# Two casting transfers in GpSimd's queue in place of eight weight copies on ScalarE, with a new hand-written order

## The chip, the cores and the metric

The kernel runs on one core of a Trainium2 chip. The metric is the device time of one execution in microseconds (us). Three runs of the kernel before took 107.3, 107.71 and 105.91 us; their median is 107.3 us. The engines are called PE (TensorE), DVE (VectorE), ACT (ScalarE), POOL (GpSimd) and SP (SyncE); PEld is PE's weight load.

## The reference

Linear attention with a polynomial feature map (4 batches, 4 heads, 1088 tokens, head dimension 32, r = 8) feeds a two-layer network with a squared ReLU:

```python
def phi(x):
    a = einsum('rd,bhsd->bhsr', S1, x)
    b = einsum('rd,bhsd->bhsr', S2, x)
    return einsum('bhsi,bhsj->bhsij', a, b).reshape(..., 64)
q_p, k_p = phi(q), phi(k)
kv  = einsum('bhsf,bhsd->bhfd', k_p, v)
z   = sum(k_p, axis=2)
num = einsum('bhsf,bhfd->bhsd', q_p, kv)
den = einsum('bhsf,bhf->bhs', q_p, z)[..., None] + 1e-06
x   = (num / den) with heads side by side: 4352 x 128
h   = x @ w_in                    # 128 x 2048
out = maximum(h, 0)**2 @ w_out    # 2048 x 128
```

All inputs and the output are float32.

## The kernel before, in words

The whole kernel is one program of about 490 named operations. A dictionary `ops` holds a function for each name, and the string `ORDER` at the head of the file lists the names; a loop at the end calls them in that order, and `keep` holds the instructions of each engine in it. So each engine runs its instructions in the order of the names, and waits by semaphore where an operand isn't ready. A second table, `BANKS`, gives the PSUM banks of each result. Both tables are written out by hand or by a planner; nothing is decided at run time.

For each batch b (0 to 3) the loads `ld_k`, `ld_q`, `ld_v` bring 544 KB each (k and q of batch 0 in three parts, v in four pieces of 32 partitions and two small rests). The names of the stages, with the lines of the profile:

- `kT`, `qT` (L338 to L341): 32x32 transposes of k and q on DVE. `kP` (L361): PE applies S1 and S2 to k; `kB` (L376): DVE transposes the result back from PSUM.
- `kp` (L381): the products of the two projections, on POOL (`kpP`) or DVE (`kpD`). `KV` (L392): PE sums k_p times v over the tokens; `KVc`, `KVt`, `KVr` (L445, L454, L460) bring that into the form that is used as a weight.
- `G` (L405), `Gc` (L423), `Wv` (L428), `Wd` (L435, L436): a small Gram matrix of the projections, from which the denominator's vector is made. For batch 0 `Ww0` (L438) and `Wc0` (L439) do it in one matrix.
- `qP` (L561; `qPa0` L540 and `qPw0` L548 for the first half of batch 0), `qB` (L571; `qBa0` L552, `qBw0` L555): the projections of q. `aw`, `dr`, `rc`, `an` (L582, L595, L596, L587): the denominator, its reciprocal and the scaled factor. `qp` (L495) and `qf` (L504): the products and their transposes. `xt` (L605) multiplies by kv and `xc` (L624, L625), or `xm` (L646) for the first half batch, writes x as bfloat16.
- The network runs in nine blocks c of 512 tokens (the last has 256). `m1_c_g` (L673) multiplies two of 16 chunks of w_in into a pair of banks, `rlA`/`rlD` (L680, L682) take the maximum with 0 on ACT or DVE, `sq`/`sqA` (L685, L688) square four chunks on DVE or ACT, `m2_c_s` (L700) multiplies four chunks by w_out. `oe` and `od` copy the block out and store it.
- `fill` (L754) issues matmuls of zeros, 384 columns wide.

The weights are loaded in float32 by SP in eight transfers (`ld_wi0` to `3`, L323; `ld_wo0` to `3`, L326) of 256 KB, and copied to bfloat16 tiles by eight ACT copies (`wiA`, L330; `woA`, L331). Their float32 tiles are not their own: `late[0]` and `late[1]` later hold k and q of the batches 2 and 3, and `w_in_f` and `w_out_f` are views of them:

```python
late = [sb(f"late{i}", [128, 2, NJ, D]) for i in range(2)]
k_in += [late[0][:, i] for i in range(2)]
q_in += [late[1][:, i] for i in range(2)]
w_in_f, w_out_f = (t.rearrange(...)[:, : CT * 128]... for t in late)
```

So `ld_k2` waits for the four `wiA`, and `ld_q2` for the four `woA`. The transfers of SP and ACT also share eight completion semaphores in turn: each waits until the eighth before it has landed.

Of the kernel before, what the change touches and what calls it, by code (L numbers as in the profile page):

```python
# [11 lines left out]
ALU = mybir.AluOpType  # L12
# [16 lines left out]
kP2 ld_v3h3 rc2 rlA_1_3 ld_v3r0 sq_0_2 m1_1_4 ld_v3r1 m2_0_1 sqA_1_0 anP2 kB2 ld_q3 m1_1_5 qpP202 qT2 m1_1_6
m2_0_2 rlA_1_4 qpP224 rlD_1_6 KV102 sqA_0_3 KV124 kpP28 KV146 qf2 KV169 qpP302 G2 kT3 KVc1 m1_1_7 qpP324 Gc2  # L30
rlA_1_5 Wv2 m2_0_3 kT3r kpP202 WdA2 qf3 rlA_1_7 qP4 KVt1 oeA0 kpP268 qB41 kP3 KVr1 od0 qB40 sqA_1_1 xt2 kB3
awP4 qT0r kpP38 dr4 G3 xcA20 rc4 m2_1_0 xcD21 Gc3 anP4 sqA_1_2 sq_1_3 m1_2_0 m1_2_1 m1_2_2 qT2r qpP502 rlA_2_0
qT1r rlD_2_1 m2_1_1 qpP524 rlA_2_2 m1_2_3 qT3 m1_2_4 kpP224 m1_2_5 rlA_2_4 m2_1_2 rlD_2_3 kpP246 rlA_2_5
m1_2_6 m1_2_7 sq_2_0 rlA_2_6 m2_1_3 rlA_2_7 m1_3_0 qpP424 oeD1 m1_3_1 rlD_3_0 Wv3 od1 m1_3_2 kpP324 rlA_3_1
m2_2_0 qf5 rlA_3_2 qpP402 m1_3_3 m1_3_4 WdA3 rlA_3_3 sq_2_1 m1_3_5 KV202 rlA_3_4 KV224 kpP346 qf4 KV246 KV269
qP6 KVc2 rlA_3_5 KVt2 qB60 m2_2_1 KVr2 qB61 sqA_3_2 xt4 sq_2_2 sq_2_3 m1_3_6 xcA40 m2_2_2 xcA41 awD6 rlA_3_6
sq_3_0 m1_3_7 m1_4_0 rlA_3_7 m1_4_1 dr6 m2_2_3 rc6 sqA_3_1 qT3r rlD_4_1 m1_4_2 m2_3_0 anD6 sq_3_3 rlA_4_0
m1_4_3 m2_3_1 rlA_4_2 qpP724 rlD_4_3 m1_4_4 sqA_4_0 m2_3_2 kpP302 rlD_4_4 m1_4_5 kpP368 m1_4_6 rlD_4_5 m1_4_7
rlA_4_6 m2_3_3 qpP702 oeD2 rlA_4_7 m1_5_0 qpP624 od2 qf7 m1_5_1 rlA_5_0 m1_5_2 KV302 sq_4_1 rlA_5_1 KV324
KV346 KV369 rlA_5_2 oeD3 m1_5_3 qpD602 od3 m1_5_4 rlA_5_3 m1_5_5 sq_4_2 m2_4_0 KVc3 qf6 KVt3 m1_5_6 KVr3  # L40
m2_4_1 rlA_5_5 rlD_5_4 m2_4_2 rlA_5_6 sq_4_3 m1_5_7 sqA_5_2 xt6 sq_5_0 m2_4_3 xcA61 xcD60 rlA_5_7 sq_5_1
m1_6_0 m1_6_1 oeA4 m1_6_2 rlA_6_0 rlD_6_1 od4 m2_5_0 rlA_6_2 m1_6_3 sq_5_3 m1_6_4 rlA_6_3 m1_6_5 rlD_6_4
m2_5_1 rlA_6_5 m1_6_6 sq_6_0 m1_6_7 m1_7_0 rlA_6_7 rlD_6_6 m2_5_2 m1_7_1 sq_6_1 rlA_7_0 m2_5_3 rlA_7_1 sq_6_3
# [747 lines left out]
```

## Time and profile before

| | |
|---|---|
| median of three runs | 107.3 us |
| profiled execution, its own time | 107.26 us |
| its span (first to last recorded instruction) | 104.9 us |
| busy: PE, DVE, ACT, POOL | 96.0, 90.4, 83.6, 40.1 us |
| read from HBM, written | 8.79 MB, 2.23 MB |
| granted PE clock | 1.00 |

The span is 2.4 us shorter than the execution's time; what lies around it is not in the trace. "Busy" of PE is modelled from pipelined matmuls, so a busy PE need not be PE at its peak. In rows of the timeline stand the start (us), the duration (us), the engine, the line, the operation, the result and operands with their shapes, and in brackets the idle time before and what ended it. "x18" counts instructions; a float32 matmul is recorded as two.

### The profile page before, as it was taken

Reading aid. Unit: us, or ns where it says so; the run is one execution under the profiler, and the core shown is the slowest. Engines: PE = TensorE matmul, PEld = TensorE weight load, DVE = VectorE, ACT = ScalarE, POOL = GpSimd, SP = SyncE. Lnnn points to the kernel's source line nnn. Section 1 sums busy time; section 2 is a strip of 40 time slices with the busy share of each in tenths; the row PEclk is TensorE's granted clock in tenths of the full one; section 3 lists DMA queues with packets and bytes.
Section 4 is the critical chain, followed back from the end, with each engine's and each line's share of the span. In section 5 each row is a group of like instructions: output and inputs, shape, how many; then the busy total and the mean of one; then the engine's idle time right before and its main releaser. Section 6 shows DMA issues by size and latency. Waiting matters only on the chain.

```text
span 104.9 us, 4069 instructions
## 1 busy us (share of the span) xinstructions
PE 96.0 (91%) x1771; PEld 69.7 (66%) x1771; DVE 90.4 (86%) x133; ACT 83.6 (80%) x105; POOL 40.1 (38%) x52
## 2 busy tenths in 40 slices
PE   2999988998889996999999999999999999999960
PEld 1436755555358853778777778877877787889950
DVE  3486598999993999999899999999999999995920
ACT  0720458499999988899999999998999799969920
POOL 4063011597099982899950008940000000210000
PEclk9999999999999999999999999999999999999999
DMA  1998999599999844000130000034102200040423
GB/s 47 284 262 289 261 395 256 104 315 232 214 254 176 198 86 112 9 0 0 31 75 6 0 6 0 0 75 99 32 6 48 52 6 0 0 106 0 103 51 106
DMA packets 9649, 11.28 MB, mean 107 GB/s; under 512 B 2592, under 2 KB 6816, under 8 KB 9632
## 3 DMA queue, kind: packets, MB, share of 16 engines
q1 hardware_dynamic: 8976, 10.59, 40.3%
q10 hardware_dynamic: 656, 0.43, 1.4%
q8 instruction: 14, 0.23, 0.9%
q14 instruction: 3, 0.02, 0.1%
HBM read 8.79 MB, written 2.23 MB: 105 GB/s over the span
## 4 chain that ended last, share of the span: by engine, by line
PE 67%; DMA 12%; DVE 9%; ACT 4%; issue 4%; SPq 0%; DVEq 0%
PE banks L700 26%; PE banks L673 23%; DMA late<-in_q_dram 8%; PE banks L605 6%; DMA k_in<-in_k_dram 3%; DVE qf L504 2%; PE banks L754 2%; PE banks L392 2%; ACT rg L680 2%; PE banks L405 2%; PE banks L361 1%; DVE qp L495 1%; DVE rg L682 1%; DVE kT L340 1%; ACT w_out_sb L331 1%
## 5 line engine op out<-in xcount | busy, mean ns | idle before, releaser
L680 ACT ACTIVATE rg<-banks 128x1024 bf16<-128x1024 f32 x50 | 48.5, 1039 | 3.2 <-PE banks L673 3.1
L673 PE MATMUL banks<-xT,w_in_sb 128*128 128x512 bf16 (+1 forms) x144 | 35.6, 371 | 0.7 <-DVE rg L682 0.4
L700 PEld LDWEIGHTS <-rg 128*128 128x128 bf16 x544 | 32.5, 98 | 5.5 <-issue 1.1
L700 PE MATMUL banks<-w_out_sb,rg 128*128 128x128 bf16 x544 | 35.3, 219 | 0.4 <-ACT rg L680 0.4
L495 POOL TENSOR_TENSOR qp<-an,qab 128x512 f32<-128x512 f32 x14 | 17.4, 1261 | 31.5 <-DVE an L587 31.3
L685 DVE TENSOR_TENSOR rg<-rg 128x2048 bf16<-128x2048 bf16 x21 | 26.0, 1250 | 0.0
L673 PEld LDWEIGHTS <-w_in_sb 128*128 128x128 bf16 x144 | 17.9, 146 | 8.2 <-issue 2.8
L682 DVE TENSOR_SCALAR rg<-banks 128x1024 bf16<-128x1024 f32 x18 | 21.6, 1209 | 1.6 <-PE banks L673 1.3
L688 ACT ACTIVATE rg<-rg 128x2048 bf16<-128x2048 bf16 x11 | 21.2, 1927 | 0.0
L381 POOL TENSOR_TENSOR kp<-kab 128x512 f32<-128x512 f32 (+1 forms) x17 | 16.2, 969 | 4.2 <-DVE kab L376 4.2
L504 DVE STREAM_TRANSPOSE qf<-qp 128x1024 f32<-128x1024 f32 (+1 forms) x9 | 10.5, 1167 | 0.0
L754 PE MATMUL banks<-zfill 128*128 128x384 bf16 x26 | 7.7, 416 | 2.0 <-POOL zfill L207 2.0
L605 PE MATMUL banks<-qf,KVr 32*32 32x256 f32 (+2 forms) x384 | 7.5, 323 | 0.8 <-DVE qab L571 0.8
L605 PEld LDWEIGHTS banks<-qf,KVr 32*32 32x32 f32 x384 | 4.7, 103 | 2.8 <-ACT KVr L460 1.3
L571 DVE STREAM_TRANSPOSE qab<-banks 128x512 f32<-128x512 f32 (+2 forms) x10 | 5.2, 550 | 0.5 <-PE banks L561 0.5
L582 POOL TENSOR_TENSOR aw<-qab 128x256 f32<-128x256 f32 (+1 forms) x3 | 1.9, 637 | 8.3 <-DVE qab L571 8.3
L754 PEld LDWEIGHTS <-zfill 128*128 128x128 bf16 x26 | 2.6, 121 | 3.5 <-POOL zfill L207 2.0
L392 PEld LDWEIGHTS banks<-kp,v_in 128*32 128x32 f32 x256 | 4.2, 116 | 0.9 <-issue 0.4
L330 ACT CAST w_in_sb<-late 128x512 bf16<-128x512 f32 x4 | 2.3, 620 | 3.0 <-DMA late<-in_moe_w_in_dram 3.0
L392 PE MATMUL banks<-kp,v_in 128*32 128x64 f32 x256 | 4.6, 227 | 0.0
L405 PEld LDWEIGHTS banks<-kab 128*64 128x64 f32 x72 | 3.1, 158 | 1.5 <-DVE kab L376 0.6
L340 DVE STREAM_TRANSPOSE qT<-late 128x1024 f32<-128x1024 f32 x2 | 2.5, 1240 | 1.8 <-DMA late<-in_q_dram 1.8
(84 smaller groups left out, 78.1 us busy)
## 6 DMA issues: line engine op xcount, KB each, us to landing
out_dram<-osb SPq DMA_DIRECT2D x32, 64.0 KB, 1.7
v_in<-in_v_dram SPq DMA_DIRECT2D x14, 128.0 KB, 8.0
late<-in_k_dram SPq DMA_DIRECT2D x2, 544.0 KB, 7.8
late<-in_q_dram SPq DMA_DIRECT2D x2, 544.0 KB, 7.8
late<-in_moe_w_in_dram SPq DMA_DIRECT2D x4, 256.0 KB, 4.3
late<-in_moe_w_out_dram SPq DMA_DIRECT2D x4, 256.0 KB, 8.3
k_in<-in_k_dram SPq DMA_DIRECT2D x1, 544.0 KB
q_in<-in_q_dram SPq DMA_DIRECT2D x1, 544.0 KB, 4.0
```

The source lines that it names most:

```text
L381: keep(eng.tensor_tensor(out=kp[i][:, m0:m1].rearrange("p m h i j -> p (m h) i j"), in0=a[:, :, :, None].to_broadcast([128, 4 * n, 8, 8]), ...
L392: keep(pe.matmul(ps[32 * h : 32 * h + 32, 0:64], v_in[b][:, h, m, :] if m < 8 else v_re[b][:, h, :], kp[i][:, m, h].rearrange("p i j -> p ...
L495: keep(eng.tensor_tensor(out=qp[i3][:, k0:k1].rearrange("p m h i j -> p (m h) i j"), in0=a[:, :, :, None].to_broadcast([128, 4 * nn, 8, 8] ...
L504: keep(dve.transpose(dst.rearrange("p g m t -> p m g t"), qp[i3][:, :n].rearrange("p m h i j -> p m (h i j)").rearrange("p m (g d) -> p m ...
L605: keep(pe.matmul(ps[:, 0:N], KVr[b if g < 8 else hi][32 * hi : 32 * hi + 32, e, 32 * h : 32 * h + 32], f[32 * hi : 32 * hi + 32, 2 * h + e ...
L673: keep(pe.matmul(y, w_in_sb.rearrange("p a b -> p (a b)")[:, per * g + z :: CT], xv, start=True, stop=True))
L680: keep(act.activation(o, pair(f"H{c}_{g}"), ACTF.Relu))
L682: keep(eng.tensor_scalar_max(o, pair(f"H{c}_{g}"), 0.0))
L685: keep(dve.tensor_tensor(out=rgs(s), in0=rgs(s), in1=rgs(s), op=ALU.mult))
L688: keep(act.activation(rgs(s), rgs(s), ACTF.Square))
L700: keep(pe.matmul(bank(f"O{c}")[:, 128 * z : 128 * z + 128], gtile(ct)[:, 128 * z : 128 * z + 128], w_out_sb[:, ct, :], start=(ct == 0 and ...
L754: keep(pe.matmul(P8[:, b, 0:384], zfill[:, 0:128], zfill, start=True, stop=True))
```

## The change

The weights are cast on the way in, by one transfer each, issued from POOL's queue straight into the bfloat16 tiles; the eight loads, the eight copies and the two views are gone:

```diff
-    for p in range(4):
-        cs = slice(4 * p, 4 * p + 4)
-        for tag, eng in (("ld", sp), ("ald", act)):
-            ops[f"{tag}_wi{p}"] = lambda cs=cs, eng=eng: keep(eng.dma_start(
-                out=w_in_f[:, cs], in_=moe_w_in.rearrange("d (ct c) -> d ct c", c=128)[:, cs]
-            ))
...
-        ops[f"wiA{p}"] = lambda cs=cs: keep(act.copy(w_in_sb[:, cs], w_in_f[:, cs]))
-        ops[f"woA{p}"] = lambda cs=cs: keep(act.copy(w_out_sb[:, cs], w_out_f[:, cs]))
+    ops["pld_wi"] = lambda: keep(pool_e.dma_start(
+        out=w_in_sb, in_=moe_w_in.rearrange("d (ct c) -> d ct c", c=128)
+    ))
+    ops["pld_wo"] = lambda: keep(pool_e.dma_start(
+        out=w_out_sb, in_=moe_w_out.rearrange("(c ct) d -> c ct d", ct=CT)
+    ))
```

The Gram matrix is made of 18 smaller matmuls for each batch, in four column groups instead of two, and its tile halves:

```diff
             for m in range(9):
-                c = m % 2
-                y = kab[i][:, m].rearrange("p r d -> p (r d)")
-                keep(pe.matmul(
-                    ps[64 * c : 64 * c + 64, 0:32], y, y.rearrange("p (h u i) -> p h u i", u=2, i=r)[:, :, 0],
-                    start=(m < 2), stop=(m >= 7),
-                ))
+                for rr_ in range(2):
+                    c = 2 * (m % 2) + rr_
+                    y = kab[i][:, m, rr_]
+                    keep(pe.matmul(
+                        ps[32 * c : 32 * c + 32, 0:16], y, y.rearrange("p (h u i) -> p h u i", h=2, u=2)[:, :, 0],
+                        start=(m < 2), stop=(m >= 7),
+                    ))
```

`fill` takes a width as well (26 fills of 384 columns become 21 of 128, 256 or 384), a form of the ReLU that no name of the order uses is added (`rlQ`), and `ORDER` and `BANKS` are new throughout. The head of the two orders, up to the first matmul of the network:

```diff
-c_id c_hm ald_S0 ld_k00 ald_S1 ld_k01 c_E c_pk c_z ald_k0r ld_v0h0 c_pW ald_v0h2 fill1b0 fill4b1 ld_v0h1 c_tab
-ald_v0h3 kT00 c_Wp fill1b2 ld_q00 ld_v0r0 c_W kP00 ld_v0r1 kT01 c_W4 ld_wi0 kT0r c_Wq kB00 kP01 ld_wi1 kpP002
-c_S2p fill2b6 kB01 c_S2c ld_wi2 G0 fill2b6 kpD024 c_pv ld_wi3 kpD046 c_eps ld_q01 Gc0 Wv0 Ww0 fill2b6 kpP08
-ld_q0r qT00 ld_k1 kpD068 qPa0 ld_wo0 Wc0 ld_wo1 qPw0 qBa0 ld_wo2 KV002 WdD0 qpD002 KV024 KV046 qpD024 ld_wo3
-wiA2 KV069 fill5b3 wiA1 qBw0 qf0 awP0 KVc0 wiA0 ld_v1h0 KVt0 fill5b3 wiA3 dr0 ld_v1h1 qT01 rc0 ld_v1h2 qP1
-rrbA KVr0 qB10 rr qB11 xt0 fill2b2 ld_v1h3 kT1 awP1 rrc kT1r xm0 ld_v1r0 woA0 kP1 xm1 dr1 m1_0_0 rc1 ld_v1r1
+c_id c_hm ald_S0 ld_k00 ald_S1 ld_k01 c_E c_pk c_z ald_k0r ld_v0h0 ald_v0h2 c_pv fill1b0w128 fill7b1w256
+ld_v0h1 c_tab c_eps ald_v0h3 kT00 c_Wp fill2b2w256 ld_q00 ld_v0r0 c_pW c_W kP00 fill1b4w256 ld_v0r1 kT01 c_W4
+pld_wi kT0r c_Wq kB00 kP01 ld_q01 kpP002 c_S2p fill4b6w256 kB01 c_S2c ld_q0r kpD024 ld_k1 pld_wo KV002 kpD046
+ld_v1h0 G0 kpP08 ld_v1h1 qT00 KV024 ld_v1h2 Gc0 kpD068 Ww0 ld_v1h3 qPa0 Wc0 Wv0 qBa0 qPw0 ld_v1r0 qT01 qpP024
+KV046 KV069 ld_v1r1 WdD0 qBw0 qP1 KVc0 awD0 qpP002 KVt0 fill6b1w384 dr0 qB10 rc0 KVr0 qB11 rrbA qf0 awP1 rr
+fill1b7w384 rrc dr1 xt0 fill3b0w384 rc1 kT1r ld_q1 anP1 kT1 qpP124 xm0 kP1 qpP102 xm1 qT0r m1_0_0 kB1 m1_0_1
```

Behind that, by the counts of the names: ReLUs on ACT 50 and then 51, on DVE 18 and then 17; squares of four chunks on ACT 11 and then 10, on DVE 21 and then 22; products `qp` on DVE for three names (`qpD002`, `qpD024`, `qpD602`) and then one (`qpD802`); `aw` on DVE for the groups 6 and 8 and then for group 0. `Wv` and `Ww0` read the smaller tile of the Gram matrix.

More of the change, by code (lines that the diff above doesn't have):

```diff
@@ L29 @@
[L29 to L33, printed above, removed]
@@ L39 @@
[L39 to L43, printed above, removed]
@@ L126 @@
     q_in += [late[1][:, i] for i in range(2)]
-    w_in_f, w_out_f = (
-        t.rearrange("p b j d -> p (b j d)")[:, : CT * 128].rearrange("p (ct c) -> p ct c", c=128) for t in late
-    )
     v_in = [sb(f"v_in{b}", [128, H, 8, D]) for b in range(4)]
@@ L136 @@
     KVs = [sb(f"KVs{i}", [128, 2, 4, 32]) for i in range(2)]
-    Gs = [sb(f"Gs{i}", [128, 32]) for i in range(2)]
+    Gs = [sb(f"Gs{i}", [128, 16]) for i in range(2)]
     KVr = [sb(f"KVr{b}", [128, 2, 128]) for b in range(4)]
@@ L437, in mk_k @@
         if b == 0:
-            ops["Ww0"] = lambda: keep(pe.matmul(bank("GW0")[:, 96:128], S2blk, Gs[i], start=True, stop=True))
+            ops["Ww0"] = lambda: keep(pe.matmul(bank("GW0")[:, 96:128], S2blk, Gs[i][:, None, :].to_broadcast([128, 2, 16]), start=True, stop=True))
             ops["Wc0"] = lambda: keep(dve.tensor_tensor(
@@ L682, in rl, with rl2 @@
                 keep(eng.tensor_scalar_max(o, pair(f"H{c}_{g}"), 0.0))
+        def rl2(g):
+            a, bb = BANKS[f"H{c}_{g}"]
+            o = rgt(g)
+            o = o if a < bb else o[:, ::-1]
+            keep(dve.tensor_scalar(o, pair(f"H{c}_{g}"), 0.0, 2.0, ALU.max, ALU.pow))
         def sq(s):
@@ L749, with fill @@
         mk_f(c)
-    def fill(n, b):
+    def fill(n, b, w):
         for _ in range(n):
-            keep(pe.matmul(P8[:, b, 0:384], zfill[:, 0:128], zfill, start=True, stop=True))
+            keep(pe.matmul(P8[:, b, 0:w], zfill[:, 0:128], zfill[:, 0:w], start=True, stop=True))
     for name in ORDER:
         if name.startswith("fill"):
-            fill(*[int(x) for x in name[4:].split("b")])
+            fill(*[int(x) for x in name[4:].replace("b", "w").split("w")])
         else:
```

60 lines of the change are left out of this document (34 added, 26 removed).

## The prediction

> **What bounds the kernel now.** I read the page first, for the shares and the slices.
>
> ```profile
> span 104.9 us, 4069 instructions
> ...
> PE 96.0 (91%) x1771; PEld 69.7 (66%) x1771; DVE 90.4 (86%) x133; ACT 83.6 (80%) x105; POOL 40.1 (38%) x52
> ...
> DVE  3486598999993999999899999999999999995920
> ACT  0720458499999988899999999998999799969920
> ...
> DMA  1998999599999844000130000034102200040423
> ```
>
> Each slice is 2.6 us. The DMA engines are full from the second slice to about 36 us; VectorE (DVE) and ScalarE (ACT) are full from about 20 us to 95 us. So there is a front part ruled by arrival and a short dependent chain, and a long part in which TensorE (PE), DVE and ACT are all full. Which of the three rules is told by the chain of work that ended last, in order of time.
>
> ```profile
> 25.20 8.87 DMA late<-in_q_dram
> ...
> 40.82 1.49 PE banks L605 x60
> 42.30 0.70 PE banks L405 x18
> 43.00 1.00 PE banks L700 x16
> ...
> 97.67 3.59 PE banks L700 x64
> 101.28 0.37 ACT osb L744
> ```
>
> From 40.82 to 101.28 us every piece of the chain is PE: 60.5 us without a hole. The last row gives 3.59 us for 64 matmuls, 56 ns for 128 columns, the same rate as everywhere else in it (16 in 0.9 to 1.0 us). This stretch gets shorter only if PE has less to do in it. Anything else must come from before 40.8 us, and there PE is not the limit:
>
> ```profile
> 0.00:5.00 5.00, 2.94 (x16) 1.33 (x24) 1.99 (x14) 1.72 (x4) 1.28 (x8) 1.00 0.59 157
> 5.00:10.00 5.00, 4.83 (x65) 2.49 (x61) 4.08 (x8) 1.07 (x7) 2.58 (x8) 1.00 1.03 283
> 10.00:15.00 5.00, 5.00 (x112) 3.29 (x111) 3.55 (x9) 2.55 (x5) 0.46 (x1) 1.00 0.94 312
> ...
> 20.00:25.00 5.00, 4.83 (x82) 3.04 (x85) 4.89 (x7) 4.79 (x7) 5.00 (x6) 1.00 0.82 261
> 25.00:30.00 5.00, 3.79 (x94) 2.31 (x84) 5.00 (x8) 5.00 (x7) 1.83 (x3) 1.00 1.10 201
> 30.00:35.00 5.00, 5.00 (x99) 3.53 (x100) 3.15 (x5) 5.00 (x6) 4.83 (x6) 1.00 0.95 200
> ```
>
> The columns are PE, PEld, DVE, ACT, POOL busy, then the granted clock, the DMA share and GB/s. From 20 to 35 us ACT is busy 14.8 of 15 us and DVE 13.0, nearly all of DVE's gap lying in one window. The waits name that gap, and what SyncE's queue waits for:
>
> ```profile
> DVE qT L340 <- DMA late<-in_q_dram: 1.8, 1, 1.8
> ```
>
> ```profile
> SPq L293 <- DMA late<-in_k_dram: 1.9, 1, 1.9
> ...
> SPq L293 <- ACT w_out_sb L331: 1.4, 1, 1.4
> ```
>
> **The change, term by term.** *The start.* The first MoE matmul (L673) starts at 19.09 us. The timeline on the way to it:
>
> ```profile
> 7.46 1.28 PE L405 MATMUL banks<-kab 128*64 128x32 f32 x18
> ...
> 9.65 0.64 PE L438 MATMUL banks<-Gs,S2blk 128*128 128x32 f32 x2
> ...
> 10.10 0.83 PE L754 MATMUL banks<-zfill 128*128 128x384 bf16 x2
> ...
> 10.86 0.68 PE L540 MATMUL banks<-qT,W 64*32 64x128 f32 x16
> ...
> 12.13 1.29 DVE L495 TENSOR_TENSOR qp<-qab 128x512 f32<-128x512 f32 x2
> ...
> 13.34 0.31 DVE L555 STREAM_TRANSPOSE qw<-banks 128x128 f32<-128x128 f32 x1
> ...
> 13.73 0.46 POOL L582 TENSOR_TENSOR aw<-qab,qw 128x128 f32<-128x128 f32 x1 [4.86 <-DVE qw L555]
> ...
> 14.70 0.26 DVE L595 TENSOR_REDUCE den<-aw 128x16 f32<-128x144 f32 x1
> 14.88 0.70 DVE L339 STREAM_TRANSPOSE qT<-q_in 128x512 f32<-128x512 f32 x1
> 15.50 0.21 DVE L596 RECIPROCAL rec<-den 128x16 f32<-128x16 f32 x1
> ...
> 16.89 1.20 DVE L340 STREAM_TRANSPOSE kT<-k_in 128x1024 f32<-128x1024 f32 x1
> ...
> 18.15 0.72 DVE L646 TENSOR_TENSOR xT<-banks,recr 128x256 bf16<-128x256 f32 x2
> ...
> 19.09 1.08 PE L673 MATMUL banks<-xT,w_in_sb 128*128 128x512 bf16 x4
> ```
>
> In the new order Wv0 and the fills no longer stand ahead of Ww0 and qPa0 (L540), while KV002 now stands ahead of G0; together I take qPa0 at 9.8 instead of 10.86. The two qp products (1.29 us) leave DVE for POOL, where they delay only qf0, and qT01 (0.70) moves into their place: qBw0 (L555) goes from 13.34 to about 11.8. aw moves from POOL to DVE and qf0 no longer stands between aw and dr0: dr0 from 14.70 to 12.4. Then qB10 takes the place of qT01, and rc0 falls from 15.50 to about 13.1: 2.4 us earlier. qf0, xt0 and kT1 follow on DVE and PE as before (kT1, 1.20 us, stands ahead of xm0 in both kernels), and since DVE now has qB11, qf0 (about 1.2), dr1, rc1, kT1r and kT1 in a row from 13.3, xm0 comes at 16.6 and L673 at 17.6. That is 1.5 us earlier, if k of batch 1 has landed by about 15.2, when DVE reaches kT1r. An earlier start does not need w_in sooner than 17.6, 14 us after its transfer is issued.
>
> Here the transfers decide. By the three windows, 157, 283 and 312 GB/s over 5 us each, 3.76 MB have come by 15 us. Up to and with k1 the queue of before holds k, v and q of batch 0, w_in and k1: four times 0.56 MB and 1.05 MB, 3.3 MB, by these rates in by 13.6 us. Afterwards both weights start early (w_in at about 3 us behind POOL's memsets, w_out behind kpP002, about 7.3) and run beside SP's queue. If all 2.1 MB get ahead of k1, it is 4.3 MB before k1: at 250 to 300 GB/s beyond 15 us that is 17 us, kT1r, kT1, xm and the first matmul follow, and L673 starts at 19.4. So the term lies between -1.5 and +0.3; I take the middle, -0.6, since w_out's second half comes late enough to fall behind k1.
>
> The same engines then carry v0 and q00 more slowly between 4 and 10 us; KV002, put ahead of G0 on PE, would hold G0 behind v0. In the worst case (w_in's 1.05 MB at 283 GB/s, 3.7 us, all in front, less what the old order already had there) qPa0 returns to about 11.8 and L673 to the same 19.4, so this is inside the same bounds and is not added.
>
> *POOL.* Each transfer costs POOL its issue. No row shows one; the nearest is SP's:
>
> ```profile
> 5.32 2.45 SPq L323 DMA_DIRECT2D late<-in_moe_w_in_dram  x4
> ```
>
> That is 0.6 us each, so I bound one between 0.3 and 2 us. Behind pld_wi waits kpP002, whose input comes only at 6.1 us: covered. Behind pld_wo waits kpP08, which only KV069 needs, some microseconds later: 0, and up to +0.5 if an issue takes 2 us. SP loses eight issues, and with them eight places among the transfers it may have open.
>
> *The eight ACT copies.*
>
> ```profile
> 17.59 1.14 ACT L331 CAST w_out_sb<-late 128x512 bf16<-128x512 f32 x2
> ...
> 24.04 1.14 ACT L331 CAST w_out_sb<-late 128x512 bf16<-128x512 f32 x2
> ```
>
> Only the pair at 24.04 lies where ACT is full; the other six lie before 20 us beside an idle ACT and are worth 0. So 1.14 us of ACT, out of 8 x 0.6.
>
> *The late loads.* q of batch 2 is issued at 25.20 because SP waits 1.4 us for w_out's last copy; it lands 8.87 us later, and DVE stands 1.8 us. The change removes the 1.4, but 8.87 us is mostly the queue (share 1.10 and 0.95 in the windows), and k3's wait (1.9 us) is for a transfer, not for a copy, so it stays. The landing moves by 0 to 2.5 us; I take 1.4 of DVE's 1.8 as won. Relu and squares can go to either engine and both are full, so PE gets its food earlier by half of the sum: (1.14 + 1.4) / 2 = 1.3. Bounds 0.6 and 1.5.
>
> *Work moved by the new order behind 20 us.*
>
> ```profile
> L680 ACT ACTIVATE rg<-banks 128x1024 bf16<-128x1024 f32 x50 | 48.5, 1039 | 3.2 <-PE banks L673 3.1
> ...
> L685 DVE TENSOR_TENSOR rg<-rg 128x2048 bf16<-128x2048 bf16 x21 | 26.0, 1250 | 0.0
> L682 DVE TENSOR_SCALAR rg<-banks 128x1024 bf16<-128x1024 f32 x18 | 21.6, 1209 | 1.6 <-PE banks L673 1.3
> L688 ACT ACTIVATE rg<-rg 128x2048 bf16<-128x2048 bf16 x11 | 21.2, 1927 | 0.0
> ```
>
> By the order's names ACT gets one relu more and one square fewer (+1.04 - 1.93), DVE one relu fewer and one square more (-1.21 + 1.25), and about 1 us of products (qpD602 at half of the 1.29 above, aw6) goes from DVE to POOL: 1.9 us off the two, 0.95 each. If PE rules throughout it is worth 0, if they rule 0.95. I take half, 0.5.
>
> *PE.* G becomes 18 small matmuls of 16 columns instead of 9 of 32. In the 43-us row above 16 issues of L700 take 1.0, and a G takes 0.70 for 18 issues; 36 issues could cost from 0.6 to 1.1 us. Two lie in the full stretch: -0.2 to +0.8, taken as 0. Fewer fills: taken as 0, with up to +0.6 (L438's 0.64 doubled) if PE ran slower for lack of them.
>
> *The sum.* -0.6 - 1.3 - 0.5 = -2.4 us. The profiled execution took 107.26 us for a span of 104.9, so 2.4 us lie around it; the median of the three runs is 107.3. Forecast: span 102.5, time 104.9 us. With every term at its best end it is -1.5 - 1.5 - 0.95 - 0.2 = -4.1, 103.2; at its worst +0.3 - 0.6 + 0.5 + 0.8 + 0.6 = +1.6, 108.9.
>
> **Rivals.** *A, interleaving eats the start.* Both weights pass ahead of k1. For it: the DMA share is already 1.03 and 0.94 from 5 to 15 us, so 2 MB pushed in there must delay something; against it: w_out is issued only after 7 us. Then +0.3 - 1.3 - 0.5 = -1.5: 105.8 us, no difference. The Trainium skill states this mechanism as a rule (DMA: Bandwidth & Descriptors, "Queues, rings and completion order"): each engine alternates between the queue rows it has work for, a packet at a time, so a second issuing engine adds no bandwidth. No run here shows two filled queues of different packet sizes yet; by that rule, with long weight rows against the 512 B pieces of q00, the sum would be A's 105.8 and not 104.9.
>
> *B, a casting transfer is slow: slower than before.* A transfer that narrows the type might move at half the rate. No row shows one. For 2.1 MB at 150 GB/s on engines that are already full, 7 us more of engine time stand ahead of q1, k2 and v1, some 4 of them ahead of k1. With 4 us of delay on A's 17 us L673 starts at 23.4: +4.3, less 0.8 for the ACT copies and half of the moved work, is +3.5, 110.8 us. It decides (over 2% slower, +2.1) from the point where L673 starts after 22.0, which is k1 landing after 19.6. Against it: w_out is not needed before the first squares, near 27 us.
>
> *C, the order is worth more.* k1 lands early, so that the start takes its best end (0.9 us more than summed), and 1.1 of the 1.4 us that PE's windows from 20 to 35 us leave empty (13.6 busy of 15) are filled: 102.9. For it: DVE and ACT have less to do there; against it: they stay full.
>
> *D, the late loads do not move at all*, since each also waits for a transfer issued before it: then the 1.4 is lost and 105.6 is left. I count it with A.
>
> **How the numbers follow.** Forecast 0.42, with its own range 103.6 to 106.2; A and D 0.20; B 0.20; C 0.18. Two per cent of 107.3 is 105.2 below and 109.4 above, about what a measurement of this kernel can tell from no change. The forecast lies just past that line, so I give it 0.26 faster and 0.16 same; with C that is 0.44 faster, with A and D 0.36 same, and B is 0.20 slower. The range reaches from 102.0 (C and a little) to 109.5 (B's milder part, and past the sum's worst end), leaving out about 0.1 above and 0.08 below.
>
> **What would show it.** Right: L673 first between 17.6 and 19.4 us; no CAST of ACT before it; DVE's wait on late q under 1 us; PE unbroken from about 39 us; G at 0.6 to 0.9 us. Wrong: kT of batch 1 waiting on k_in (A, B), weights landing after 16 us (B), holes in PE's chain after 41 us (then the new order, not PE's work, sets the end), or PE's part after 41 us shorter by more than 1 us.

## The result and the profile after

The changed kernel took 111.28 us (median of four runs, 109.34 to 113.29) beside 107.39 us for the kernel before (four runs). The ratio is 1.029, with a 95% interval of 1.020 to 1.037: slower, where 104.9 us and a gain were forecast. A ratio here compares the runs of each kernel that lie close to its fastest, a median is over all its runs, and a profile is of one run, whose own time stands in the table below: what is read from a profile far above its kernel's fastest run need not hold for the ratio. The profiled run took 110.51 us for a span of 108.7, so 1.8 us lie around the span (2.4 before).

The page of the changed kernel, its span, PE's clock and the DMA share in 40 slices, and the two queues that matter (packets, MB, share of 16 engines):

```profile
span 108.7 us, 4176 instructions
...
PEclk9999555599999999999999999999999999999996
DMA  2999999999960000210030000003400031200341
...
q0 software_dynamic: 288, 1.05, 5.0%
...
q8 instruction: 14, 0.23, 0.8%
```

Before, PEclk was 9 throughout; now it is 5 in four slices, from about 11 to 22 us. The loads are all in after 12 slices, 33 us, where before they lasted to about 41. PE's own timeline says where the 3.8 us of span went:

```profile
9.63 0.43 PE L382 MATMUL banks<-kp,v_in 128*32 128x64 f32 x16 [1.80 <-DMA v_in<-in_v_dram]
...
12.25 0.68 PE L531 MATMUL banks<-qT,W 64*32 64x128 f32 x16 [1.20 <-DVE qT L328]
...
16.51 0.74 PE L552 MATMUL banks<-qT,Wq 32*32 32x128 f32 x32 [1.75 <-DVE Wq L427]
...
17.66 2.13 PE L753 MATMUL banks<-zfill 128*128 128x384 bf16 x6
19.58 1.06 PE L626 MATMUL banks<-ident,rec 128*128 128x128 f32 x4
...
23.33 2.38 PE L664 MATMUL banks<-xT,w_in_sb 128*128 128x512 bf16 x9
...
31.74 0.47 PE L382 MATMUL banks<-kp,v_in 128*32 128x64 f32 x17 [1.57 <-issue]
```

The first matmul of the network (L664, before L673) starts at 23.33 us instead of 19.09: 4.24 us late. From it to the last piece of the chain it is 104.60 - 23.33 = 81.3 us, where before it was 101.28 - 19.09 = 82.2. So in this profile the whole loss lies in the start, and behind it 0.9 us are won; the end from that piece on is 0.5 us longer (4.1 beside 3.6).

```profile
...
5.41 10.26 DMA q_in<-in_q_dram
...
17.87 1.92 PE banks L753 x6
...
53.06 2.86 ACT rg L671 x3
55.92 1.80 ACT rg L686
...
59.95 2.98 ACT rg L671 x3
62.95 1.91 ACT rg L686
...
104.60 0.37 ACT osb L743
```

The longest row of the chain names the start's cause in this run: the second part of q of batch 0 (q01) is issued at 5.41 us and takes 10.26 us to come. DVE stands for both parts, q00 and q01; the first row is the kernel before, where q00 was in time at 8.31 us:

```profile
8.31 0.70 DVE L338 STREAM_TRANSPOSE qT<-q_in 128x512 f32<-128x512 f32 x1
```

```profile
11.48 0.71 DVE L328 STREAM_TRANSPOSE qT<-q_in 128x512 f32<-128x512 f32 x1 [2.47 <-DMA q_in<-in_q_dram]
...
15.69 0.71 DVE L329 STREAM_TRANSPOSE qT<-q_in 128x512 f32<-128x512 f32 x1 [2.20 <-DMA q_in<-in_q_dram]
...
17.74 0.21 DVE L587 RECIPROCAL rec<-den 128x16 f32<-128x16 f32 x1
```

What shared the engines with it is seen in the DMA view from 2 to 18 us, where the two casting transfers (q0) hold a third of the 16 engines, and in POOL's timeline, which shows when they were issued:

```profile
q1 hardware_dynamic: 3768, 2.60, 60.9%
q0 software_dynamic: 288, 1.05, 33.7%
...
w_in_sb<-in_moe_w_in_dram POOLq DMA_DIRECT2D x1, 512.0 KB, 8.0
q_in<-in_q_dram SPq DMA_DIRECT2D x2, 256.0 KB, 8.9
```

```profile
2.83 0.72 POOL L316 DMA_DIRECT2D w_in_sb<-in_moe_w_in_dram  x1
...
7.21 0.59 POOL L319 DMA_DIRECT2D w_out_sb<-in_moe_w_out_dram  x1
```

The parts of q took 8.9 us (middle of the two) from issue to landing; before it was 4.2. In the trace a packet of the casting queue is 4096 bytes and took 299 ns of an engine on average, one of the 512-byte packets of SP's queue 29 ns. With little to do from 8 us on, PE also lost its clock (the columns are those of the prediction's windows: PE, PEld, DVE, ACT, POOL busy, then the granted clock, the DMA share, GB/s):

```profile
10.00:15.00 5.00, 3.52 (x131) 2.52 (x118) 1.84 (x4) 0.35 (x2) 1.43 (x2) 0.61 1.03 259
15.00:20.00 5.00, 3.49 (x42) 2.11 (x43) 4.14 (x13) 1.08 (x3) 1.19 (x3) 0.50 0.97 236
20.00:25.00 5.00, 4.95 (x95) 2.80 (x95) 3.47 (x6) 1.57 (x3) 3.06 (x4) 0.87 1.05 273
...
30.00:35.00 5.00, 3.38 (x104) 2.34 (x94) 4.22 (x6) 3.61 (x6) 0.72 (x2) 1.00 0.38 111
```

At 0.50 the six fills take 2.13 us and `rr` (L626) 1.06; before, `rr` (L635) took 0.66. A last thing is new: at 30.17 us PE stops inside a group of matmuls for 1.57 us, and the trace shows nothing that it waits for ("issue").

### The profile page after: what moved, and what is told of

It reads as the page before. It is cut to its first block, busy times and chain, and to the rows that moved or that the text cites. A ratio compares the mean times of both kernels' runs of the same rounds, so it can differ in the third digit from the quotient of the medians.

```text
span 108.7 us, 4176 instructions
## 1 busy us (share of the span) xinstructions
PE 94.4 (87%) x1827; PEld 69.7 (64%) x1843; DVE 90.6 (83%) x129; ACT 78.7 (72%) x98; POOL 43.8 (40%) x57
## 3 DMA queue, kind: packets, MB, share of 16 engines
q0 software_dynamic: 288, 1.05, 5.0%
## 4 chain that ended last, share of the span: by engine, by line
PE 65%; DMA 12%; ACT 12%; issue 4%; SPq 1%; DVE 1%
PE banks L698 25%; PE banks L664 23%; DMA q_in<-in_q_dram 9%; ACT rg L671 6%; PE banks L596 6%; ACT rg L686 3%; PE banks L753 3%; DMA k_in<-in_k_dram 3%; PE banks L552 2%; PE banks L351 2%; PE banks L382 1%; PE banks L445 1%; PE banks L396 1%; SPq L303 1%; ACT xT L615 1%
## 5 line engine op out<-in xcount | busy, mean ns | idle before, releaser
L664 PE MATMUL banks<-xT,w_in_sb 128*128 128x512 bf16 (+1 forms) x128 | 33.9, 372 | 0.9 <-ACT rg L671 0.3
L683 DVE TENSOR_TENSOR rg<-rg 128x2048 bf16<-128x2048 bf16 x22 | 27.6, 1273 | 0.0
L664 PEld LDWEIGHTS <-w_in_sb 128*128 128x128 bf16 x144 | 17.6, 147 | 7.0 <-issue 2.0
L673 DVE TENSOR_SCALAR rg<-banks 128x1024 bf16<-128x1024 f32 x17 | 20.4, 1209 | 0.6 <-PE banks L596 0.4
L371 POOL TENSOR_TENSOR kp<-kab 128x512 f32<-128x512 f32 (+1 forms) x17 | 17.9, 1079 | 4.8 <-DVE kab L366 4.8
L686 ACT ACTIVATE rg<-rg 128x2048 bf16<-128x2048 bf16 x10 | 19.1, 1940 | 0.1
L486 POOL TENSOR_TENSOR qp<-an,qab 128x512 f32<-128x512 f32 x14 | 15.6, 1140 | 5.8 <-DVE an L578 5.6
L573 POOL TENSOR_TENSOR aw<-qab 128x256 f32<-128x256 f32 (+2 forms) x5 | 3.8, 768 | 32.6 <-DVE qab L562 32.6
L753 PE MATMUL banks<-zfill 128*128 128x256 bf16 (+2 forms) x26 | 7.5, 427 | 2.1 <-POOL zfill L203 2.0
L436 ACT COPY KVs<-banks 128x256 f32<-128x256 f32 x4 | 1.4, 385 | 5.4 <-PE banks L382 5.4
L552 PE MATMUL banks<-qT,Wq 32*32 32x256 f32 (+2 forms) x160 | 3.4, 360 | 1.8 <-DVE Wq L427 1.8
L366 DVE STREAM_TRANSPOSE kab<-banks 128x576 f32<-128x576 f32 (+2 forms) x5 | 3.3, 663 | 1.8 <-PE banks L351 1.8
```

The source lines that it names most:

```text
L371: keep(eng.tensor_tensor(out=kp[i][:, m0:m1].rearrange("p m h i j -> p (m h) i j"), in0=a[:, :, :, None].to_broadcast([128, 4 * n, 8, 8]), ...
L486: keep(eng.tensor_tensor(out=qp[i3][:, k0:k1].rearrange("p m h i j -> p (m h) i j"), in0=a[:, :, :, None].to_broadcast([128, 4 * nn, 8, 8] ...
L664: keep(pe.matmul(y, w_in_sb.rearrange("p a b -> p (a b)")[:, per * g + z :: CT], xv, start=True, stop=True))
L673: keep(eng.tensor_scalar_max(o, pair(f"H{c}_{g}"), 0.0))
L683: keep(dve.tensor_tensor(out=rgs(s), in0=rgs(s), in1=rgs(s), op=ALU.mult))
L686: keep(act.activation(rgs(s), rgs(s), ACTF.Square))
```

## The experiments

Theory 1: the early casting transfers take engine time from q and v of batch 0, whose arrival the new order has on its path. Rivals: the casting itself is slow; the new order is slow by itself; the low clock is the cause and not a consequence. A second theory came from the first runs: PE stops because the next piece of its own program comes late. Each profile gave a start of the network, the stops of PE of 0.5 us or more, and a length from that start to the last piece of the chain, the last copy. The column "profile" has the profiled run's own time and its mean granted clock:

| kernel | median us (runs) | ratio, 95% | profile: us, clock | network starts | PE's stops ("issue") | start to last copy |
|---|---|---|---|---|---|---|
| before | 107.39 (4) | | 107.26, 1.00 | 19.09 | none | 82.2 |
| after | 111.28 (4) | 1.029 [1.020, 1.037] | 110.51, 0.94 | 23.33 | 1.57 | 81.3 |
| e1_late_weights | 107.73 (10) | 1.000 [0.995, 1.005] | 108.67, 0.97 | 19.91 | 1.87, 1.85 | 82.8 |
| e2_before_cast | 108.99 (4) | 1.015 [1.012, 1.019] | 109.08, 1.00 | 21.57 | 0.93 | 81.4 |
| e3_plain_weights | 108.72 (10) | 1.002 [0.996, 1.009] | 110.94, 0.97 | 20.45 | 0.94, 2.00 | 85.1 |
| e4_no_weights | 109.14 (10) | 0.998 [0.991, 1.005] | 109.08, 0.96 | 22.29 | 2.65, 1.27 | 81.0 |
| e5_fills | 109.25 (4) | 1.023 [1.014, 1.033] | 108.49, 1.00 | 21.03 | 0.99, 0.65, 0.92 | 81.6 |
| e6_plain_pool | 109.34 (4) | 1.025 [1.014, 1.036] | 109.21, 0.97 | 22.38 | 0.51 | 81.3 |
| e7_later_wout | 109.34 (4) | 1.015 [1.004, 1.026] | 110.05, 0.97 | 20.83 | 2.69, 1.65 | 83.3 |
| e8_before_late_cast | 107.15 (10) | 1.007 [1.003, 1.010] | 106.28, 1.00 | 19.11 | none | 81.0 |
| e9_old_gram | 108.73 (4) | 1.016 [1.009, 1.023] | 108.25, 0.97 | 17.84 | 1.38 | 84.3 |
| e10_only_win_early | 112.07 (4) | 1.048 [1.042, 1.053] | 111.87, 0.98 | 21.91 | 0.72, 2.35 | 84.1 |
| e11_few_fills | 108.43 (10) | none (see there) | 108.73, 0.97 | 18.64 | 1.47, 2.69 | 84.2 |
| e12_no_late_loads | 106.13 (12) | 0.994 [0.988, 1.000] | 105.94, 1.00 | 19.01 | none | 81.0 |

The kernel before was run again beside each group of kernels, and the ratios are to these runs: its medians were 107.54 us (e1, e2, e3, e5), 106.94 (e4, e6, e7, e8), 106.80 (e9, e10, e11) and 107.62 (e12).

**Late weights.** The two casting transfers only move back in POOL's queue, to about 8.6 and 13 us:

```diff
-pld_wi kT0r c_Wq kB00 ... ld_k1 pld_wo KV002 kpD046
+kT0r c_Wq kB00 ... ld_k1 KV002 kpD046
-kpP08 ld_v1h1 ... qpP002 KVt0
+kpP08 pld_wi ld_v1h1 ... qpP002 pld_wo KVt0
```

> The changed kernel with the two casting transfers later in POOL's order: w_in behind kpP08 (about 8 us) instead of ahead of kpP002 (2.8 us), w_out behind qpP002 instead of ahead of kpP08 (7.2 us). Theory 'starved inputs' (the casting transfers share the DMA engines with v0, q00 and q01, which the start needs first): q00 lands near 8 us and q01 near 10 instead of 11.5 and 15.7, the first matmul of the network (L664) starts between 17.6 and 19.0 instead of 23.3, PE's granted clock stays at 1.0, and the time is 105 to 107. Rival 'order' (the new order is slow by itself: KV002 ahead of G0, qT01 on the way to rc0, fewer fills): L664 still after 21 and the time 109.5 or more.

The time went back to that of the kernel before (1.000), though neither it nor the start reached the ranges expected. q00 and q01 were transposed at 9.01 and 10.70 us without a wait, and `rc0` came at 13.40 where the prediction's chain had 13.1:

```profile
10.70 0.67 DVE L328 STREAM_TRANSPOSE qT<-q_in 128x512 f32<-128x512 f32 x1
...
13.40 0.21 DVE L586 RECIPROCAL rec<-den 128x16 f32<-128x16 f32 x1
```

So the early place of the two transfers was the cause of the loss, and the chain on DVE had been worked out rightly up to `rc0`. Yet the network began at 19.91, not at 17.6. PE's timeline:

```profile
13.84 0.40 PE L551 MATMUL banks<-qT,Wq 32*32 32x128 f32 x3 [1.87 <-issue]
...
14.45 1.89 PE L752 MATMUL banks<-zfill 128*128 128x384 bf16 x6
16.13 1.06 PE L625 MATMUL banks<-ident,rec 128*128 128x128 f32 x4
...
19.91 1.30 PE L663 MATMUL banks<-xT,w_in_sb 128*128 128x512 bf16 x4
```

PE stopped for 1.87 us three matmuls before the end of the projections `qP1`, and then ran six fills in 1.89 us in front of `rr`, at a granted clock of 0.69 from 15 to 20 us. The one packet of the program's queue in the DMA view from 10 to 15 us took 1.8% of 16 x 5 us, 1.4 us; it landed at 12.42 us, and PE went on at 13.84:

```profile
q8 instruction: 1, 0.02, 1.8%
```

**The casting alone, in the old order**, at the same early places of POOL's queue:

```diff
-c_z ald_k0r
+c_z c_pv c_eps pld_wi ald_k0r
-kpP002 c_S2p
+kpP002 pld_wo c_S2p
-(ld_wi0 to 3, ld_wo0 to 3, wiA0 to 3, woA0 to 3)
```

> The kernel before, in its own order, with only the weights changed: the eight loads and eight copies are gone and the two casting transfers stand in POOL's queue where the changed kernel has them (2.8 us, behind the memsets, and behind kpP002). 'Starved inputs': q00 lands near 11.5 instead of 8.1, so qPa0 moves from 10.9 to 12.3; q01 lands at 15.7, when the old order wants it at 14.9; L673 starts at 20.5 to 21.5 instead of 19.1 and the time is 107.5 to 109.5. 'Order': no harm from the transfers, L673 at 19.1 or sooner and 105.5 to 106.5.

It costs 1.5% here, and 108.99 us is in the range expected: q00 comes at 11.28 us after a wait of 1.99, while q01, which the old order transposes only at 16, is never waited for. So the early transfers cost in either order. They cost more in the new one (2.9%), but that this is q01's place is not shown: three kernels below lose 2.3 to 4.8% with q01 transposed at 13.1 to 13.5 us without a wait.

**The new order with the old eight loads and copies:**

```diff
-pld_wi ... pld_wo
+ld_wi0 ld_wi1 ld_wi2 ld_wi3 (behind ld_v0r1) ... ld_wo0 ld_wo1 ld_wo2 ld_wo3 (behind ld_k1)
+wiA2 wiA1 (behind Gc0) wiA0 wiA3 (KVc0) woA0 woA1 (rrc) woA3 woA2 (Gc1)
```

> The changed kernel in its new order, with only the weights undone: eight float32 loads in SP's queue at the places of the kernel before (behind v_re, behind k1) and eight ACT copies, into the tiles of the late k and q. 'Starved inputs': all of batch 0 but q01 comes as early as before, L664 starts at 18 to 19.5 and the time is 106 to 108. 'Order': L664 after 21 and the time 109.5 or more, since nothing that this theory blames is undone.

Ratio 1.002; its ten runs scatter from 106.48 to 110.94, and their median and the start miss the ranges expected (q01 is waited for here too, for 2.02 us, to 12.70). The order by itself brings no gain that can be seen.

**No weight transfers at all.** The two tiles are set to 0 on DVE, so the weights are left out and the output is 0:

```diff
-pld_wi ... pld_wo
+c_w0 (behind c_pk): memset(w_in_sb, 0.0), memset(w_out_sb, 0.0)
```

> The changed kernel without any transfer of weights: both weight tiles are set to zero on DVE at the start, so its output is zero and its time shows what the new order can do when nothing shares the DMA engines with q, k and v. 'Starved inputs': q00 lands by 8 us and q01 by 9.5; L664 starts between 17.5 and 19.5 and the time is 104 to 106.5. 'Order': L664 still after 21, time 109 or more. If L664 comes at 19 to 20 with all inputs in time, the start that the prediction worked out (17.6) left something out that stands on PE's own queue, the fills ahead of the reciprocal's transposes.

Even with 2.1 MB less to read the ratio is 0.998 (ten runs, 106.07 to 113.31): all of q was in time (9.06 and 11.34 us, no wait), but the start of the profiled run was ruined by a stop of 2.65 us in `qP1` and half clock behind it. Its 22.29 us and the median are the figures expected of the rival 'order', and came by something that neither theory had. So more than the weights was in the way.

**Fifteen more fills in the changed kernel**, to keep PE's clock up:

```diff
+fill5b0w384 (behind c_S2c) fill4b0w384 (behind Ww0) fill6b1w384 (behind KV069)
```

> The changed kernel with 15 more fills of 384 columns on PE where it stood idle (5 ahead of KV002, 4 behind Ww0, 6 behind KV069). PE's granted clock should then stay at 1.0 from 10 to 21 us, where it was 0.5. If the low clock is a cause of its own: the reciprocal's transposes and fills (L626, L753) from 17.7 to 20.6 us take 1.5 us less, L664 starts near 21.8 and the time is 109.5 to 110. If it is only a symptom of the late inputs: L664 within 0.4 us of 23.3 and the time unchanged, 110.9 to 111.5.

The clock stayed at 1.00 and the median fell by 2.0 us to 109.25, still 2.3% above before:

```profile
16.14 0.46 PE L551 MATMUL banks<-qT,Wq 32*32 32x128 f32 x18 [0.99 <-issue]
...
21.03 1.30 PE L663 MATMUL banks<-xT,w_in_sb 128*128 128x512 bf16 x4
```

So the low clock is not the first cause, but it lengthens the start: the six fills in front of `rr` take 1.14 us here instead of 2.13, and from `rc0` to `xm0` it is 3.26 us instead of 4.40. `rc0` itself came only 0.75 us sooner, though q01 came 2.5 us sooner in this profile (13.20 us, no wait): the stop of 0.99 us lies between them. That the fills make the whole kernel faster is not shown: the ratios, 1.023 and 1.029, have overlapping intervals, and the changed kernel's shortest run, 109.34 us, had a mean granted clock of 0.992 without them.

**POOL's queue without casting:** the same two issues move float32 into the old tiles, and ACT copies.

```diff
-    out=w_in_sb, in_=moe_w_in...      # and w_out_sb
+    out=w_in_f, in_=moe_w_in...       # and w_out_f, with the eight ACT copies
```

> The changed kernel with its two transfers from POOL's queue at the same places and in the same two pieces, but without the cast: float32 into the tiles of late k and q, then eight ACT copies. If the second queue's interleaving does the harm, q00 and q01 land as late as in the changed kernel (near 11.5 and 15.7), L664 starts at 22.5 to 24 and the time is 110 to 112.5. If the cast is what is slow, q01 lands by 13, L664 starts before 21 and the time is 107 to 109.

The loss stays (1.025), and so does the wait for q00; the start and the time lie just under the ranges of the first theory:

```profile
DVE qT L334 <- DMA q_in<-in_q_dram: 2.4, 1, 2.4
```

The cast is not needed for the loss. q01, expected near 15.7, was transposed at 13.50 us without a wait, so the long wait for it in the changed kernel's profile is not needed either; q00's late landing is what both have. What they share is two large early transfers in a queue of their own: the same floats in eight loads of SP's queue, in the same order, gave 1.002. Whether the queue or the size of the transfers does it was not tried.

**w_out later still**, behind `qpP124`:

```diff
-qpP002 pld_wo KVt0
+qpP002 KVt0 ... qpP124 pld_wo xm0
```

> e1_late_weights with w_out still later, behind the first product of unit 1 (POOL near 18 us instead of 12.9). The first squares need it near 29 us. 'Starved inputs' with the share of instruction loads: the PE pause of 1.9 us inside qP1 (from 12.0 us in e1, while a 16 KB instruction packet is on the way) depends on the load of the DMA engines; with less of it L664 starts at 18.5 to 19.5 instead of 19.9 and the time is 106 to 107. If the pause is the program's own, L664 stays at 19.9 and the time at 107 to 107.7, or grows if w_out then comes late for the first m2.

The stop in `qP1` remained (2.69 us, up to 14.79), though w_out was issued only at 18.86 us. The stop does not come from w_out's load. Both ranges are missed: the time is no better than with the earlier place (1.015 beside 1.000).

**The old order with late casting transfers:**

```diff
+kpP08 pld_wi ld_q0r ... awP0 pld_wo KVc0
-(ld_wi0 to 3, ld_wo0 to 3, wiA0 to 3, woA0 to 3)
```

> The kernel before in its own order, eight copies and eight loads gone, the casting transfers placed where they meet few early inputs: w_in behind kpP08 (near 9 us), w_out behind the first aw (near 14). 'Starved inputs': nothing is late any more, L673 within 0.5 us of 19.1, and the 1.1 us of ACT and the wait for late q are won: 105.3 to 106.8, a ratio of 0.98 to 0.995. If the old order's time hangs on the copies in no way: 107 to 107.7.

It does what the prediction's term of -1.3 us was about: the copies are gone, the late q is not waited for, and DVE's gap from 30 to 35 us is closed (4.97 busy, before 3.15):

```profile
30.00:35.00 5.00, 4.95 (x110) 3.73 (x114) 4.97 (x7) 5.00 (x5) 4.82 (x6) 1.00 0.25 70
```

In the profile the stretch behind the start is 1.2 us shorter (81.0 against 82.2). Over ten runs the time is not: 107.15 beside 106.94, ratio 1.007. The profile is of the shortest of these ten runs (106.28, the others 106.83 to 107.87), beside a middle one of the kernel before (107.26), so its 1.2 us are no gain of the change that is shown.

**The stops of PE, tried.** Counted over the timeline's rows from the start, PE's stops lie behind 221, 348, 474, 599 or 1103 matmuls, in both orders and in eleven kernels (a few records can be missing from a trace; the stop behind 348 is one of 0.28 us in the old order). In the kernel with 15 more fills ahead, the first stop lay 15 matmuls earlier in `qP1` (18 before its end instead of 3). The places are thus about 126 matmuls, or multiples of it, apart, each matmul being two instructions. The page's 14 packets of 0.23 MB are 16 KB each, and 0.23 MB over the 3670 recorded matmuls and weight loads is 63 bytes each, so a packet holds some 260 of them. The Trainium skill says the same (Runtime: NRT & Kernel Launch, "Instruction fetch mechanics": refills in 16 KiB blocks of 256 instructions by a DMA queue of the engine's own), but calls the cost "mostly hidden"; the stops of 0.51 to 2.69 us here were not. At each of the 19 stops in the table a packet of this queue landed 1.3 to 1.7 us before PE went on, and had begun 2.4 to 3.0 us before it. The next kernel is the one with late weights, with the Gram matrix of before:

```diff
-                for rr_ in range(2):
-                    c = 2 * (m % 2) + rr_
-                    y = kab[i][:, m, rr_]
...
+                c = m % 2
+                y = kab[i][:, m].rearrange("p r d -> p (r d)")
```

> The kernel of the experiment with both casting transfers late (107.73 us, first matmul of the network at 19.91 us, PE pausing 1.87 us three records before the end of the projections qP1), with the Gram matrix made again by 9 matmuls of 32 columns for each batch (18 records fewer for each G on PE). If PE stops at a fixed place in its instruction stream, because the next piece of its program has not arrived, the pause moves 18 records on: out of qP1 and into the 64 records of xt0 (L595), and qP1 ends without a hole. If instead it stops at a fixed time, because something in the memory or in the results' banks holds it near 12 us, the pause stays in qP1. The time stays between 107.0 and 108.2 us under both.

The stop left `qP1`, as the fixed place wants; in `xt0`, where it was expected, there is none, since the packet had landed at 13.77 us, 1.7 us before PE came to the place (15.50). The second stop, again behind 474 matmuls, moved on from `KV1` into `qP2`. The network now began at 17.84 us, close to the prediction's best end of 17.6, and with all ten fills: PE had run six of them before `rec` was there, and waited 1.00 us for it. But the time was 108.73, outside what I had expected, since all was lost again from 25 to 35 us:

```profile
12.58 1.14 PE L751 MATMUL banks<-zfill 128*128 128x384 bf16 x6
14.71 0.66 PE L624 MATMUL banks<-ident,rec 128*128 128x128 f32 x4 [1.00 <-ACT rec L620]
...
17.84 2.38 PE L662 MATMUL banks<-xT,w_in_sb 128*128 128x512 bf16 x9
...
27.61 0.66 PE L550 MATMUL banks<-qT,Wq 32*32 32x256 f32 x14 [1.38 <-issue]
```

```profile
25.00:30.00 5.00, 3.34 (x73) 1.58 (x63) 3.97 (x6) 2.97 (x4) 0.73 (x1) 0.92 1.09 251
30.00:35.00 5.00, 5.00 (x51) 3.42 (x50) 2.34 (x7) 3.54 (x5) 3.54 (x4) 0.74 0.62 138
```

The stop lets ACT and DVE run dry, then the clock falls to 0.74, and the stretch behind the start is 84.3 us.

**Only w_in early** (the changed kernel with `pld_wo` behind `qpP002`):

```diff
-pld_wo KV002 kpD046
+KV002 kpD046 ... qpP002 pld_wo KVt0
```

> The changed kernel with w_in's transfer in its early place and only w_out's moved behind qpP002. If the early share of w_in in the transfers is what delays q of batch 0 (q01's request stands open from 5.4 us, w_in's packets lie beside it until 10.8), q00 still lands after 10.5 and q01 after 13, the first matmul of the network comes after 21.5 us, and the time is 109.0 to 110.5. If w_out (issued at 7.2 us) does it, q00 still lands late but q01 lands by 12, the first matmul comes by 20.7 and the time is 107.5 to 108.5.

The start is where theory 1 put it (21.91), with q00 at 11.16 after a wait of 1.82 and q01 at 13.08 without one. So the early place of w_in alone is enough for the late start. The time missed both ranges: with 112.07 us it is the slowest of all; the second stop is 2.35 us and the stretch 84.1.

```profile
31.09 0.47 PE L381 MATMUL banks<-kp,v_in 128*32 128x64 f32 x17 [2.35 <-issue]
```

**Few fills** (late weights, 2 fills instead of 10 in front of the network):

```diff
-KVt0 fill6b1w384 ... rr fill1b7w384 ... xt0 fill3b0w384
+KVt0 fill2b1w384 ... rr ... xt0
```

> The kernel with both casting transfers late, with 8 of the 10 fills (384 columns) taken away that stand in PE's queue between KVt0 and the first matmul of the network: 2 instead of 6 ahead of rr, none in place of 1 and 3. If the fills stand on the path, rr comes at once after rec (about 15.2 instead of 16.13), the first matmul comes 0.7 to 1.7 us earlier than 19.91, and the time falls to 106.0 to 107.2. If the fills hold up the granted clock, it falls below 0.6 from 14 to 20 us, the matmuls there take twice as long, and the first matmul comes no earlier than 19.9, the time 107.5 to 109.

`rr` came at 15.38 and the network at 18.64, 1.27 us earlier: where PE comes late to those fills, they stand on the path. The second stop lay 8 matmuls further on, 9 instead of 17 before the end of the same group, as 8 matmuls fewer ahead of it want, and was longer:

```profile
28.49 0.35 PE L381 MATMUL banks<-kp,v_in 128*32 128x64 f32 x9 [2.69 <-issue]
```

Ten runs scatter from 105.40 to 112.11, so no ratio is given. The median, 108.43, is that of the second theory and the start that of the first; the clock was 0.66 from 15 to 20 us, beside 0.69 with the fills, so they had not held it up.

**No late loads.** The kernel with the old Gram matrix, without the loads of k, q and v of batches 2 and 3, whose tiles are filled in places where POOL and ACT are idle; half of the output is not the reference's:

```diff
-ld_k2 ld_v2h0 ... ld_q2 ld_k3 ld_v3h0 ... ld_q3
+c_l0 (memset late0) c_l1 c_l2 c_l3 (copies of k0) c_l4 (memset v3)
```

> The kernel of the experiment with late casting transfers and the old Gram matrix (108.73 us; first matmul of the network at 17.84 us; PE stops for 1.38 us inside qP2 at 26.23, and the granted clock is 0.74 from 30 to 35 us), with the loads of k, q and v of the batches 2 and 3 left out (3.26 MB; the tiles are filled by two memsets of GpSimd, three small ones, and three copies on ScalarE at places where both are idle, so half of the output is not the reference's). If the next piece of PE's program comes late because the 16 DMA engines are full, they are empty from about 21 us, the pause near 26 us is gone (under 0.3 us), the clock stays at 1.00 from 25 to 35 us, and the early start is kept: 104.5 to 106.2 us. If the piece comes late whatever else is moving, or the clock falls for another reason, the pause of 1 us or more and the clock under 0.9 stay, and the time is 107.3 to 109.

```profile
25.00:30.00 5.00, 4.77 (x156) 3.33 (x154) 5.00 (x7) 4.62 (x7) 1.48 (x2) 1.00 0.02 5
30.00:35.00 5.00, 5.00 (x74) 3.53 (x71) 4.47 (x9) 5.00 (x5) 3.54 (x4) 1.00 0.01 3
```

With the DMA engines empty (share 0.02 instead of 1.09) no stop is left, the clock is 1.00, and the stretch behind the start is 81.0 instead of 84.3 us; the ratio is 0.994 beside 1.016 for the same kernel with its loads. The packet that PE stopped for there began at 25.05 us, when PE had begun 456 matmuls; here it began at 24.34 us, behind 345. So at this place the program's next piece was late because the 16 engines were full. The early start was not kept (19.01): G of batch 0 took 1.28 us here and 0.77 there, why I have not traced.

Full engines are not the whole of it. In the kernel with 15 more fills PE stopped behind 1103 matmuls, from 54.13 us, with the engines at a share of 0.56 and then of 0.03 and 0.00; the packet came from 52.56 to 53.68 us, and the 76 matmuls up to the place took PE only 1.57 us:

```profile
52.00:53.00 1.00, 1.00 (x80) 1.00 (x76) 1.00 (x2) 1.00 (x2) 1.00 (x1) 1.00 0.56 148
53.00:54.00 1.00, 1.00 (x60) 0.56 (x48) 1.00 (x2) 1.00 (x1) 1.00 (x2) 1.00 0.03 4
54.00:55.00 1.00, 0.14 (x10) 0.00 (x0) 0.84 (x3) 1.00 (x3) 0.97 (x1) 1.00 0.00 0
```

```profile
55.05 0.65 PE L551 MATMUL banks<-qT,Wq 32*32 32x256 f32 x12 [0.92 <-issue]
```

And the kernel before, whose engines were as full, had no stop behind 474 matmuls: from its packet's start (26.34 us) PE took 4.50 us to the place, through 41 matmuls, eight of them 512 columns wide, and two short waits. The changed kernel's packet began at 28.85 us, and PE was there after 1.32 us, through 62 narrow ones. So what counts, as far as these traces show, is whether PE gets to the end of the piece before it sooner than 2.4 to 3.0 us after the packet's start. What sets that start is not in the traces.

No kernel that computes the whole reference was faster than the one before. Late transfers take away the wait for q00, but they are not all: with both of them late the new order is at 1.000 (late weights), 1.015 (w_out later still) and 1.016 (old Gram matrix), and what sets these apart is not shown.

## Why the prediction was wrong, point by point

- **The start, -0.6 forecast, +4.24 measured.** The failing step is "Here the transfers decide", with its bounds -1.5 and +0.3. I summed bytes up to k1 and let k1 alone decide; k1 was never waited for. The landing of q00 and q01 was put at nothing by the sentence "this is inside the same bounds and is not added". In the profile qPa0 came at 12.25, 2.45 us behind the chain's 9.8; the new order had put qT01 into the chain ahead of qBw0, and it waited 2.2 us more, to 15.69, so that rc0 came at 17.74 instead of 13.1; and from rc0 to xm0 it was 4.4 us instead of 3.5, behind fills at a clock of 0.50. These make 5.5 of the 5.7 us between 17.6 and 23.33. All four kernels of the new order with w_in's transfer at its early place (this one, more fills, no cast, only w_in early) have the late q00, at 10.79 to 11.80 us, beside 8.93 to 9.20 in the seven others; of the four this one alone waits for q01.
- **The clock and the fills.** "Fewer fills" was taken as 0, with +0.6 at worst. There are not fewer: 26 before and after (the 21 given with the change is wrong), 15 of them narrower. The clock fell to 0.50 where PE had 3.5 of 5 us to do, which cost the start some 1.1 us (3.26 instead of 4.40 from rc0 to xm0 with more fills); in the ratios (1.023 and 1.029) it does not show clearly.
- **The best end of 17.6** left out the arrival of PE's program and what follows when PE comes late: the fills in front of `rr` then stand on the path (1.92 us of the changed kernel's chain, 1.27 for eight of them with late weights). At full speed the chain held: in the three kernels whose six fills took 1.14 to 1.20 us (fifteen more fills, old Gram matrix, no late loads), rc0 and xm0 lie 3.25 to 3.26 us apart, beside 3.5 forecast, and one of them began the network at 17.84. There nothing was won all the same: the end of the chain depends on 25 to 35 us as much as on the start.
- **POOL's issues, 0:** right. They took 0.72 and 0.59 us and were covered.
- **Copies and late loads, -1.3:** the loads did come in 8 us sooner and DVE's wait for the late q is gone, but ten runs of the old order with just this gave no gain (1.007).
- **Moved work, -0.5, and G, 0:** behind the start 0.9 us were won in the profile in spite of a stop of 1.57. But PE's chain did not stay unbroken, as the prediction wanted: from 53.06 to 65.83 us it is ACT's relus and squares that stand in it, but for one short piece of PE. G itself became cheaper: 36 issues take 0.50 us, against 0.6 to 1.1 feared. Its 18 more records for each batch move the groups in which PE comes to the end of a piece of its program.
- **Rivals.** A had the right mechanism, two filled queues, and the wrong price (105.8): it too looked at k1 only. With the rule of the Trainium skill cited with it (DMA: Bandwidth & Descriptors, "Queues, rings and completion order") the trace agrees as far as shares can tell: both queues were served side by side, 33.7% to the casting one. B is refuted: 1.05 MB written in 5.0% of the engines' time, and the loss is the same without casting. Its time of 110.8 was near by luck, and its sign, weights landing after 16 us, came for another reason (w_out took 10.0 us from 7.21). C fell with the start, and D too: the late loads did move.

## What to carry to other kernels

Here, while the DMA engines were full, large transfers issued early were paid for by the small loads issued next to them (8.9 us instead of 4.2 for a part of q), so price the landing of every load that the new order has put on its path, not only of the last one. A chain that is worked out to tenths must take in all that stands in the engine's queue, fillers too, for when the engine comes late to them. And a gain at the start counts only if the stretch behind it is not waiting for something else; a diagnostic kernel without the suspected loads shows that quickly.

## What the runs showed of the hardware

PE's instructions come in pieces of 16 KB through the same DMA engines as the data (14 packets, 0.23 MB, in each profile). PE can stop for 0.5 to 2.7 us at a fixed count of instructions, about 126 matmuls or a multiple of it apart, with "issue" as the only sign in the profile; at all 19 such stops it went on 1.3 to 1.7 us after a packet had landed. Full engines made the packet late in the one pair tried (456 matmuls begun instead of 345), but many small matmuls brought PE to the place too soon even without them (0.92 us at a DMA share of 0.56, then 0), and slower work in front of it hid the packet in the kernel before (4.50 us instead of 1.32). Taking 36 matmuls out ahead of the second place moved the stop there from one group into another.
